# A new order for an attention stage, with three small steps of its first head pair put behind that pair's low parts

## The chip, the cores and the metric

The kernel runs on one core of a Trainium2 chip. The metric is the device time of one launch, in microseconds (us). The median of three runs before the change is 432.57 us (430.47 to 432.88).

The core has five engines that each work through their own list of instructions in the order in which the program was built, and wait for one another by semaphores: PE (matrix products and transposes), ACT (activations, copies, casts), DVE (elementwise work and reductions), POOL (elementwise work, constants, and transfers with computed addresses) and SP, which here only issues transfers. A long wait at the head of a list holds up all that stands behind it.

## The reference, cut to what matters

Three parts follow each other, all in float32:

```python
# 1. attention with a linear memory: B=2, H=8 heads, S=576 rows, D=64
scores = scale * q @ k.T ; causal ; a = softmax(scores) ; local = a @ v
q_p = where(q > 0, q, exp(q) - 1) + 1
mem = (q_p @ M_prev) / (q_p @ z_prev + 1e-6)
x = sigmoid(beta) * mem + (1 - sigmoid(beta)) * local       # 1152 tokens x 512

# 2. a mixture of 8 experts: each token goes to its best expert, at most 288 each
e = argmax(x @ w_gate) ; x = gate_w * relu(x @ w1[e]) @ w2[e]

# 3. a gated block
out = ((x @ w_a) * (x @ w_b)) @ w_out
```

## The kernel before, in words

**Work and stages.** The first stage holds the attention, the gate, and all of the expert with most tokens of the first batch. A branch on the counts follows, and the second stage computes the other experts and the gated block. Numbers are split into a high and a low part, and a product of two such numbers is three products on PE.

**The attention.** Heads are taken in pairs, eight pairs numbered 0 to 7. For each pair n the steps are: turn the queries (PE, step `qt`, line 428, into a PSUM tile `psS`), write their high part (ACT, `qh`, line 452) and low part (DVE, `ql`, line 466), a rectified copy (ACT, `qr`, line 457) and an exponential (ACT, `qe`, line 462) for the memory; POOL caps the exponential (`qm`, line 480) and adds the two (`qp`, line 486). Keys are turned (`kt`, line 428) and split (`kh`, line 494 on ACT; `kl`, line 498 on DVE). From pair 1 on, POOL copies parts side by side (`dq`, lines 513 to 517; `dk`, line 522) and SP moves the rest between partitions (`d`, line 505). `mm` (line 527) are the memory's products.

Each pair has five score tiles (n, 0) to (n, 4), of growing width. A tile goes through scores `S` (PE, lines 568 and 584), minimum and mask `M` (DVE, line 600), exponential `E` (ACT, line 620), transposes `T` (PE, line 635), copies out of PSUM `V` (ACT, lines 646 and 652), products with the values `P` (PE, lines 662 and 699), a turn back `X` (line 673, after the copy `os` of line 667) and the final scaling on DVE. There are two `psS` tiles in all: turned queries, turned keys, memory products and scores share them. Where ACT and DVE both read one PSUM tile, the build makes the second engine wait for the first.

**Small constants** (lines 365 to 375, step `small`): ACT takes the exponential of beta, DVE makes gate factors from it in four short instructions (lines 367 to 370), PE turns z, and DVE copies it into the memory's operand `mb` (line 374). The first `mm` needs it.

**What sets the order.** `Plan` (line 111) holds every step with an engine, a cost, what it follows, a key and the tiles it takes. `run` (line 150) plays the steps against these costs; of those that could start about first on an engine it takes the one with the least key. A key is the pair number plus the entries of `KEYS` (line 23) for that kind of step; `late` is how long after its end a step's result counts as there. Instructions are then emitted in that order, so the table sets the order of every engine's list. The order of the second stage comes from another table.

**Other traffic of the first stage.** Ten steps `z` (line 1100) clear the token buffer `xs_d` and the output in DRAM from SP; the first also fills `id_d` (line 422), 128 x 9 elements of 4 bytes. For batch 0, after pair 3, the gate's steps choose experts (`g1` to `g4`, lines 719 to 808), weigh the rows (line 781) and scatter them into `xs_d` (`g5`, line 813, on POOL). The first expert's tokens come back as `x0t` (line 951, SP).

Of the kernel before, what the change touches and what calls it, by code (L numbers as in the profile page):

```python
# [19 lines left out]

ABUFS = 3
SVB = 3
KEYS = dict(E=502, E_=221, F=-302.1, F_=64, L=118.7, M=-967.5, M_=566.5, N=-316.3, N_=50.2, O=-50.5, O_=-139, P=675.4,
            P_=-121.7, S=327, S_=188.6, T=-56.2, T_=-185.4, V=-77.6, V_=-123.1, X=-248.6, X_=66.4, consts=613.8,
            cv=-172.7, d=-43.2, e1=-207.9, e2=269, ec=1026.2, eh=-418.9, ep=113.4, ex=-759.2, ey=332.5, g1=274.3,
            g1_=-394.9, g1b=-306.3, g1b_=-110.1, g2=67.8, g2_=-153, g2b=51.5, g2b_=-136.7, g3=-413.3, g3_=-237.4,
            g4=-39.8, g4_=118, g4b=-451.8, g4b_=-214.9, g5=18.9, ge=-74.6, ge_=-163.6, gw=687.7, gw_=40.6, kh=-4.2,
            kl=149.6, kt=-65.6, last=69.9, mm=-247.7, mm_=1082, mn=-147.5, mo=188.3, mo_=401, pad0=-71.5, pad1=18.1,
            pb=101.2, pw=3.2, px=-43.8, qd=64.4, qe=-113.3, qh=-114.8, ql=-307.9, qm=31.9, qp=-222.9, qr=158.8,
            qt=-196.2, tc=219.1, tot=410.5, tr=-407.9, w=221.9, w_=92.1)  # L30
GK = 0.0
AHEAD_ = 0.132
CHANGE = 0.25
UNITS = [0, 1, 2, 3, 4]
ON_DVE = []
# [161 lines left out]
def fused_kernel(  # L197
# [256 lines left out]
    def q_relu(n):  # L454
        d = st[n]
        d["ph"] = ap2.tile([128, 128 * NT], F32, tag="ph", name="ph", bufs=1)
        nc.scalar.activation(out=d["ph"][:, 0:S], in_=d["qT"], func=AF.Relu)

    def q_exp(n):
        d = st[n]  # L460
        d["eq"] = ap2.tile([128, S], F32, tag="eq", name="eq", bufs=1)
        nc.scalar.activation(out=d["eq"], in_=d["qT"], func=AF.Exp)
# [6 lines left out]
    def q_stack(n):  # L469
        for h in range(2):  # L470
            me = slice(64 * h, 64 * h + 64)
            to = slice(64 * h, 64 * h + 64)
            src = st[n]["s"][me, 1, 128 * NF_:S] if n else st[n]["d"][me, h, 1, 128 * NF_:S]
            nc.gpsimd.tensor_copy(out=qd[sched.got["qd", n][1]][me, to], in_=src)
            if n == 0:
                nc.gpsimd.tensor_copy(out=qd[2][me, to], in_=st[n]["d"][me, h, 0, 128 * NF_:S])

    def q_min(n):
        eq = st[n]["eq"]
        nc.gpsimd.tensor_scalar(out=eq, in0=eq, scalar1=1.0, scalar2=None, op0=ALU.min)  # L480
# [507 lines left out]
    def work(name, engine, cost, do, after=(), key=(0, None), takes=(), uses=(), late=None, mode=0):  # L988

        at_, what = key  # L990
        keys = [] if what is None else [what] + ([what + "_"] if at_ >= LAST * UP and what + "_" in KEYS else [])
        meta.append((at_, keys, name))
        missing = [a for a in after if a not in op]
        assert not missing, (name, missing)
        op[name] = sched.add(engine, cost, do, [op[a] for a in after], at_ + sum(KEYS[k_] for k_ in keys), takes, uses,
                             LATES[engine] if late is None else late, 0, mode)

    def there(name, takes=(), late=0.0):
        work(name, "SP", 0.0, lambda: None, key=(-99, None), takes=takes, late=late)
# [9 lines left out]

    for n in range(min(2, len(pairs))):  # L1010
        for j, w in enumerate("qkv"):
            there(("load", n, w), [(w, (w, n))], (5.2, 7.9, 8.5, 9.5, 10.5, 11.5)[3 * n + j])
    there("d0", [("d", ("d", 0))])
    work("at first", "POOL", 5.5, lambda: None, (), (-99, None))
    for name, cost, do in (("last", 1.9, last_tile_constants), ("pad1", 1.2, lambda: padding(1)),
                           ("pad0", 1.2, lambda: padding(0)), ("consts", 3.6, gate_constants)):
        work(name, "POOL", cost, do, ["at first"], (0, name))
    there("zr", late=9.0)
    work("small", "PE", 0.2, small_constants, ["zr"], (-6, None), [("C", "small")], late=0.4)
    ZP = 10  # L1020
    for n, (b, p) in enumerate(pairs):
        at_ = n * UP
        if n > 1:
            for w in "qkv":
# [3 lines left out]
             [("q", n)])  # L1028
        work(("qh", n), "ACT", 0.531 if n else 1.06, lambda n=n: q_high(n), [("qt", n)], (at_, "qh"), (),
             [("qT", n), ("s", n)])  # L1030
        work(("qr", n), "ACT", 0.531, lambda n=n: q_relu(n), [("qt", n)], (at_, "qr"), (), [("qT", n), ("ph", n)])
        work(("qe", n), "ACT", 0.531, lambda n=n: q_exp(n), [("qt", n)], (at_, "qe"), (), [("qT", n), ("eq", n)])
        work(("ql", n), "DVE", 0.669 if n else 1.34, lambda n=n: q_low(n), [("qh", n)], (at_, "ql"), (),
             [("qT", n), ("s", n)])
        work(("qd", n), "POOL", 1.1, lambda n=n: q_stack(n), [("ql", n), "last"], (at_, "qd"), [("qd", ("qd", n))], [("s", n)])
        work(("qm", n), "POOL", 1.75, lambda n=n: q_min(n), [("qe", n)], (at_, "qm"), (), [("eq", n)])
        work(("qp", n), "POOL", 1.45, lambda n=n: q_phi(n), [("qm", n), ("qr", n)], (at_, "qp"), (),
             [("eq", n), ("ph", n)])
        work(("kt", n), "PE", 0.111 * NT, lambda n=n: k_turn(n), [("load", n, "k"), ("qt", n)], (at_, "kt"),
             [("S", ("kT", n))] + ([] if n else [("C", "stir2")]), [("k", n)])  # L1040
        work(("kh", n), "ACT", 0.531, lambda n=n: k_high(n), [("kt", n), ("qh", n)], (at_, "kh"), (),
             [("kT", n), ("s", n)])
        work(("kl", n), "DVE", 0.669, lambda n=n: k_low(n), [("kh", n)], (at_, "kl"), (), [("kT", n), ("s", n)])
        ready = [("ql", n), ("kl", n)]
        if n:
            work(("dq", n), "POOL", 2.75, lambda n=n: q_beside(n), [("qh", n), "pad0", "pad1"], (at_, "d"), [("d", ("d", n))], [("s", n)])
# [182 lines left out]
    if FAST:  # L1229
        if WA0:  # L1230
            for n, half in enumerate("sd"):
                def words_ahead(n):
                    c = sched.got["wa", n]
                    held_cells["raw", ("ff", "a", 0), n] = "raw", len(raws) + 2 * n + c[1]
                    load_words(raw_half(*c), w_a[:, 0:512], n)

                work(("wa", n), "SP", 2.92, lambda n=n: words_ahead(n), [("qt", LAST), ("d", LAST)], (tk, "pw"),
                     [(half, ("wa", n))], late=2.0)
        for j in range(NF):
            def block_ahead(j):  # L1240
                c = held_cells["raw", ((PRE_R, 0), PRE_R, 1, j)] = sched.got["pre", j]
                load_block(raws[c[1]], PRE_R, 1, j)

            work(("pre", j), "SP", 2.92, lambda j=j: block_ahead(j), ["rank"] + [("lo", NF + j_, 1) for j_ in range(NF)],
                 (tk, "pb"), [("raw", ("pre", j))], late=2.0)

        def tokens_ahead():
            c = sched.got["prex"]
            held_cells["xs", (PRE_R, 0)] = "raw", len(raws) + c[1]
            load_tokens(token_rows(raw_half(*c)), PRE_R, 0, 160 if PRE_R == NBIG - 1 else SW, nc.sync)  # L1250

        work("prex", "SP", 1.0, tokens_ahead, ["rank"] + [("g5", t) for t in range(L0, NTT)], (tk, "px"), [("s", "prex")],
             late=2.0)
        work("end", "", 0.0, lambda: None, ["prex", "totals", ("e", "yl", KD - 1)] + [("pre", j) for j in range(NF)] +
             [("wa", n) for n in range(2 * WA0)], (tk, None), (),
             ["prex"] + [("pre", j) for j in range(NF)] + [("wa", n) for n in range(2 * WA0)])
# [601 lines left out]
```

## Time and profile before

| what | us |
|---|---|
| median of three runs | 432.57 |
| the profiled execution | 430.72 |
| its span, first to last instruction | 428.9 |
| first scores of pair 0 begin | 10.78 |
| first scores of pair 2 begin | 47.78 |
| last product of the first stage begins | 177.19 |
| first work of PE in the second stage | 181.91 |

The profiled execution is 1.8 us longer than its span, and 1.85 us shorter than the median. PE is busy 398.1 us of the span, DVE 267.0, ACT 206.8 and POOL 103.9. Times in the rows are counted from the start of the span. In a row of the timeline the first number is the start, the second the time from the first to the last of the merged instructions, and what stands in brackets is how long the engine had been idle and what ended that.

### The profile page before, as it was taken

How to read it: one execution, taken by the hardware profiler on the slowest of the kernel's cores; microseconds unless marked ns; L12 is line 12 of the kernel's file. 1: busy time of each engine (PE TensorE's matmuls, PEld its weight loads, DVE VectorE, ACT ScalarE, POOL GpSimd, SP SyncE). 2: the span in 40 equal slices, each digit the busy share in tenths (PEclk: the TensorE clock that was granted, in tenths of full speed). 3: DMA queues.
4: the chain of work that ended last, by engine and by line, in shares of the span. 5: the costliest groups of instructions: out<-in, count | busy, mean ns of one | idle time of the engine just before them, and what ended most of it. 6: DMA issues, size and time to landing. Idle time of an engine off the chain costs nothing.

```text
span 428.9 us, 7838 instructions
## 1 busy us (share of the span) xinstructions
PE 398.1 (93%) x2860; PEld 348.3 (81%) x2860; DVE 267.0 (62%) x640; ACT 206.8 (48%) x451; POOL 103.9 (24%) x181
## 2 busy tenths in 40 slices
PE   5699889999989999589999989999999999999993
PEld 5678778887778999588998878898778987878892
DVE  5668678568997486256720128899957679743231
ACT  4388689687896452055711135354643354122010
POOL 6486745552830003300000000005700000000302
PEclk9699999999999997969999999999999999999998
DMA  5549899861996001779998999945960000000201
GB/s 134 131 106 138 172 297 252 244 199 54 307 288 232 2 3 59 250 277 387 387 385 314 378 397 407 383 166 135 165 127 2 0 2 1 0 2 0 97 4 62
DMA packets 59910, 74.46 MB, mean 174 GB/s; under 512 B 33955, under 2 KB 33955, under 8 KB 59856
## 3 DMA queue, kind: packets, MB, share of 16 engines
q1 hardware_dynamic: 58016, 70.48, 53.4%
q0 software_dynamic: 1632, 3.31, 2.3%
q8 instruction: 26, 0.43, 0.5%
q14 instruction: 28, 0.23, 0.2%
q10 hardware_dynamic: 208, 0.01, 0.0%
HBM read 58.75 MB, written 11.64 MB: 164 GB/s over the span
## 4 chain that ended last, share of the span: by engine, by line
PE 64%; DVE 8%; POOL 8%; issue 7%; DMA 6%; ACT 4%; ACTq 0%; SPq 0%; POOLq 0%
PE bank L954 10%; PE bank L955 9%; PE bank L956 9%; PE bank L1687 4%; PE bank L1688 4%; PE bank L1689 4%; PE bank L1547 3%; DMA id_d<-far 3%; PE bank L1454 3%; PE psB L954 2%; DVE sv L600 2%; PE psB L956 2%; PE bank L1490 2%; PE psB L955 2%; DMA raw<-in_moe_w_dram 2%
## 5 line engine op out<-in xcount | busy, mean ns | idle before, releaser
L954 PE MATMUL bank<-x,part 128*128 128x512 f32 (+1 forms) x192 | 66.7, 348 | 0.4 <-ACT x L966 0.4
L955 PE MATMUL bank<-x,part 128*128 128x512 f32 (+1 forms) x192 | 66.6, 347 | 0.0
L620 ACT ACTIVATE a<-sv,mn 128x128 f32<-128x128 f32 (+4 forms) x72 | 41.7, 584 | 17.9 <-DVE mn L600 17.2
L813 POOL DMA_INDIRECT id_d<-tid,dsi x10 | 13.6, 1362 | 116.6 <-DVE dsi L907 113.9
L954 PEld LDWEIGHTS bank<-x,part 128*128 128x128 f32 x192 | 36.1, 188 | 5.0 <-issue 0.6
L955 PEld LDWEIGHTS bank<-x,part 128*128 128x128 f32 x192 | 36.1, 188 | 4.2
L600 DVE CUSTOM_DVE_ANT_0 sv<-psS,mask 128x128 f32<-128x128 f32 (+4 forms) x72 | 34.4, 515 | 5.7 <-PE psS L584 4.1
L635 PE MATMUL psB<-ident,a 128*128 128x128 f32 x200 | 30.9, 278 | 2.7 <-ACT a L620 2.6
L956 PE MATMUL bank<-x,part 128*128 128x512 f32 (+1 forms) x96 | 33.3, 347 | 0.0
L956 PE MATMUL bank<-x,xt 128*128 128x512 f32 (+1 forms) x96 | 33.3, 346 | 0.0
L635 PEld LDWEIGHTS psB<-ident,a 128*128 128x128 f32 x200 | 23.5, 143 | 6.0 <-ACT a L620 4.3
L966 ACT CAST part<-u 128x1024 fp32r<-128x1024 f32 x18 | 18.7, 1050 | 18.2 <-DVE u L1371 14.9
L969 DVE TENSOR_TENSOR x<-bank,x 128x160 f32 (+3 forms) x12 | 4.2, 367 | 36.6 <-ACT x L966 36.6
L652 ACT COPY at<-psB 128x512 f32<-128x512 f32 (+2 forms) x48 | 23.6, 510 | 6.4 <-PE psB L635 6.3
L1663 ACT COPY c<-bank 128x512 f32<-128x512 f32 (+1 forms) x24 | 11.8, 499 | 25.7 <-PE bank L956 21.4
L1666 DVE TENSOR_TENSOR c<-c,bank 128x512 f32<-128x512 f32 (+1 forms) x24 | 13.8, 577 | 16.0 <-PE bank L956 11.0
L813 POOL DMA_INDIRECT out_dram<-c,ids x4 | 4.0, 988 | 80.8 <-DVE c L1697 79.0
L966 ACT CAST a<-c 128x512 fp32r<-128x512 f32 (+1 forms) x12 | 6.4, 534 | 35.4 <-DVE c L1666 28.8
L662 PE MATMUL psC<-at,ldv 128*64 128x256 f32 (+1 forms) x192 | 20.0, 350 | 0.5 <-ACT at L652 0.4
L813 POOL DMA_INDIRECT xs_d<-x,di x10 | 10.4, 1036 | 41.2 <-DVE ggt L774 37.0
L956 PEld LDWEIGHTS bank<-x,xt 128*128 128x128 f32 x96 | 18.0, 188 | 2.1
L956 PEld LDWEIGHTS bank<-x,part 128*128 128x128 f32 x96 | 18.0, 188 | 2.1
(281 smaller groups left out, 1081.9 us busy)
## 6 DMA issues: line engine op xcount, KB each, us to landing
raw<-in_moe_w_dram SPq DMA_DIRECT2D x16, 1024.0 KB, 8.2
raws<-in_moe_w_dram SPq DMA_DIRECT2D x6, 1024.0 KB, 10.6
rawd<-in_moe_w_dram SPq DMA_DIRECT2D x6, 1024.0 KB, 13.6
xs_d<-h SPq DMA_DIRECT2D x10, 512.0 KB, 4.8
raw<-in_moe_w_b_dram SPq DMA_DIRECT2D x4, 1024.0 KB, 13.8
d<-s SPq DMA_DIRECT2D x14, 288.0 KB, 4.0
rawd<-in_moe_w_a_dram SPq DMA_DIRECT2D x3, 1024.0 KB, 19.0
raws<-in_moe_w_out_dram SPq DMA_DIRECT2D x3, 1024.0 KB, 12.4
```

The costliest lines, as they stand in the source:

```text
L600: nc.vector.tensor_tensor_reduce(out=o, in0=i0, in1=i1, scale=1.0, scalar=3.0e38, op0=ALU.add, op1=ALU.min, accum_out=mn[:M])
L620: nc.scalar.activation(out=st[u, "a"][:M, h, 0:W], in_=sv[:M, 0:W], func=AF.Exp, scale=-1.0, bias=mn[:M], **more)
L635: nc.tensor.transpose(pt[:kr, M * j:M * j + M], a_t[:M, h, 128 * kt:128 * kt + kr], ident[:M, :M])
L652: eng(out=st[n, a, "at"][:, h0:h0 + nh, 0:i + 1, c0:c0 + 128], in_=pt[:, 0:m * 128].rearrange("p (h k m) -> p h k m", h=nh, m=128))
L662: nc.tensor.matmul(po[64 * h:64 * h + 64, c0:256], lhsT=vt[:, kt, h, 0:D], rhs=at_[:, h, kt, c0:256], start=kt == 0, stop=kt == 2 * a + 1)
L813: ins = nc.gpsimd.indirect_dma_start(out=out_[:, :], out_offset=bass.IndirectOffsetOnAxis(ap=idx, axis=0), in_=in_, in_offset=None, bounds ...
L954: nc.tensor.matmul(out_, lhsT=wh, rhs=xh, start=first, stop=False)
L955: nc.tensor.matmul(out_, lhsT=wh, rhs=xl, start=False, stop=False)
L956: nc.tensor.matmul(out_, lhsT=wl, rhs=xh, start=False, stop=last)
L966: nc.scalar.copy(out=to, in_=src)
L1687: nc.tensor.matmul(o, lhsT=g[:, 0, ts_], rhs=wh[:, m, :], start=m == 0, stop=False)
L1688: nc.tensor.matmul(o, lhsT=g[:, 0, ts_], rhs=wl[:, m, :], start=False, stop=False)
```

## The change

Three edits, all in the first stage's steps.

1. For pair 0, `qr` and `qe` now also follow `ql` and `kh`, and the step `small` follows `kl` (before, it came first of all, with key -6). In the source the steps of `qr`, `qe`, `qd`, `qm` and `qp` stand behind `kl`.
2. Planning figures: the keys of pair 0 count as there at 7.2 instead of 7.9, the result of `small` 2.5 instead of 0.4 after its end, and the step that loads tokens for the second stage has cost 1.6 and 3.5 after it, instead of 1.0 and 2.0.
3. All values of `KEYS` and `AHEAD_` are new.

```diff
-            qt=-196.2, tc=219.1, tot=410.5, tr=-407.9, w=221.9, w_=92.1)
+            qp=-218.7, qr=-108.5, qt=-332.6, tc=405.9, tot=85.8, tr=1033.4, w=515.2, w_=-76.2)
-AHEAD_ = 0.132
+AHEAD_ = 0.023
...
-            there(("load", n, w), [(w, (w, n))], (5.2, 7.9, 8.5, 9.5, 10.5, 11.5)[3 * n + j])
+            there(("load", n, w), [(w, (w, n))], (5.2, 7.2, 8.5, 9.5, 10.5, 11.5)[3 * n + j])
-    work("small", "PE", 0.2, small_constants, ["zr"], (-6, None), [("C", "small")], late=0.4)
...
-        work(("qr", n), "ACT", 0.531, lambda n=n: q_relu(n), [("qt", n)], (at_, "qr"), (), [("qT", n), ("ph", n)])
-        work(("qe", n), "ACT", 0.531, lambda n=n: q_exp(n), [("qt", n)], (at_, "qe"), (), [("qT", n), ("eq", n)])
...
+        first = [("ql", 0), ("kh", 0)] if n == 0 else []
+        work(("qr", n), "ACT", 0.531, lambda n=n: q_relu(n), [("qt", n)] + first, (at_, "qr"), (), [("qT", n), ("ph", n)])
+        work(("qe", n), "ACT", 0.531, lambda n=n: q_exp(n), [("qt", n)] + first, (at_, "qe"), (), [("qT", n), ("eq", n)])
...
+        if n == 0:
+            work("small", "PE", 0.2, small_constants, ["zr", ("kl", 0)], (-6, None), [("C", "small")], late=2.5)
...
-        work("prex", "SP", 1.0, tokens_ahead, ["rank"] + [("g5", t) for t in range(L0, NTT)], (tk, "px"), [("s", "prex")],
-             late=2.0)
+        work("prex", "SP", 1.6, tokens_ahead, ["rank"] + [("g5", t) for t in range(L0, NTT)], (tk, "px"), [("s", "prex")],
+             late=3.5)
```

What it moves is shown at three places.

**The start.** ACT, from the high part of pair 0's queries (L452) to its first score tiles (L620); before:

```order
L452 ACTIVATE d_76<-psS 64x576 x2
L462 ACTIVATE eq<-psS 128x576
L457 ACTIVATE ph<-psS 128x576
L494 CAST s_74<-psS 128x576
L366 ACTIVATE rg<-bet 128x8
L620 ACTIVATE a,sums<-sv,mn 128x128 x2
```

and now:

```order
L452 ACTIVATE d_76<-psS 64x576 x2
L494 CAST s_74<-psS 128x576
L462 ACTIVATE eq<-psS 128x576
L457 ACTIVATE ph<-psS 128x576
L620 ACTIVATE a,sums<-sv,mn 128x128
L366 ACTIVATE rg<-bet 128x8
```

The keys' high part (L494) has moved from fourth to second place, and beta's exponential (L366) between the two halves of the first score tile. DVE at the same place, before:

```order
L466 SCALAR_TENSOR_TENSOR d_76<-psS,d_76 64x576 x2
L367 TENSOR_SCALAR rg<-rg 128x8
L368 RECIPROCAL rog<-rg 128x8
L369 TENSOR_SCALAR rog<-rog 128x8
L370 RECIPROCAL rog<-rog 128x8
L374 COPY mb<-psC 64x8 x2
L498 TENSOR_TENSOR s_74<-psS,s_74 128x576
L600 ISA sv,mn<-psS,mask 128x128
```

and now:

```order
L466 SCALAR_TENSOR_TENSOR d_76<-psS,d_76 64x576 x2
L498 TENSOR_TENSOR s_74<-psS,s_74 128x576
L600 ISA sv,mn<-psS,mask 128x128
L600 ISA mn 128x1
...
L367 TENSOR_SCALAR rg<-rg 128x8
L368 RECIPROCAL rog<-rg 128x8
L369 TENSOR_SCALAR rog<-rog 128x8
L370 RECIPROCAL rog<-rog 128x8
L374 COPY mb<-psC 64x8 x2
L600 ISA sv,mn<-psS,mask 128x256
```

The constants (L367 to L374) no longer stand ahead of the keys' low part (L498), but between the minima of tiles (0, 0) and (0, 1).

**The first clearing transfers.** SP's list around them (`d_76<-s_74` is the move of pair 2, `ldv_82` its values), before:

```order
L281 DMA ldk_80<-in_k_dram 128x4x64 x2
L284 DMA ldk_80<-in_k_dram 64x2x64
L417 DMA xs_d<-h_97 128x2x512
L422 DMA id_d<-far 128x9x1
L505 DMA d_76<-s_74 64x1152 x2
L281 DMA ldv_82<-in_v_dram 128x4x64 x2
```

and now:

```order
L281 DMA ldk_80<-in_k_dram 128x4x64 x2
L284 DMA ldk_80<-in_k_dram 64x2x64
L505 DMA d_76<-s_74 64x1152 x2
L417 DMA xs_d<-h_97 128x2x512
L422 DMA id_d<-far 128x9x1
```

The move of pair 2 stands ahead of the clearing now, and three clearing steps follow each other behind it; the loads of pair 5 and the move of pair 3 come behind these.

**The gate of batch 0.** POOL's list around the five scatters (L813), before (pair 7's copies, `d_77`):

```order
L517 COPY qz_99<-s_75 64x64
L522 COPY d_77<-s_75 64x576 x2
L813 DMA xs_d<-x_95,di 2560x512 x5
L480 TENSOR_SCALAR eq<-eq 128x576
L485 MEMSET ph 128x64
```

and now (pair 6's copies, `d_76`):

```order
L486 TENSOR_TENSOR ph<-eq,ph 128x576
L474 COPY qd_138<-s_74 64x64 x2
L813 DMA xs_d<-x_95,di 2560x512 x5
L522 COPY d_76<-s_74 64x576 x2
L474 COPY qd_139<-s_75 64x64 x2
```

The scatters have moved from behind the last copy of pair 7 to ahead of the last copy of pair 6. On SP the load of `x0t` stands accordingly earlier, behind the first block of the first expert's weights and ahead of the second.

PE's list has the same products, all in all, up to the first scores of pair 2, in another order: all transposes and products of pair 0 now stand ahead of the scores of pair 1, and so do pair 2's turned queries and keys. At the first stage's end, 96 instead of 72 products of the first expert follow the last count of the gate (L840).

## Rows read from the trace of the kernel before

**Rows 1.** Windows: stretch, then busy time (instructions) by engine, granted clock, DMA.
```profile
10.00:20.00 10.00, 6.47 (x33) 6.03 (x33) 5.81 (x22) 3.68 (x13) 3.62 (x11) 0.66 0.62 137
20.00:30.00 10.00, 8.86 (x63) 7.52 (x63) 6.57 (x23) 8.09 (x22) 9.26 (x36) 1.00 0.50 121
40.00:47.78 7.78, 6.33 (x55) 4.63 (x53) 4.38 (x14) 5.50 (x13) 3.56 (x7) 1.00 0.92 61
47.78:177.50 129.72, 123.61 (x952) 111.22 (x952) 95.34 (x353) 85.92 (x219) 49.26 (x73) 0.97 0.60 186
```
**Rows 2.** Timeline of the start, pair 0 up to its first score tiles.
```profile
5.97 1.30 ACT L452 ACTIVATE d<-psS 64x576 fp32r<-64x576 f32 x2 [3.66 <-PE psS L428]
7.97 1.54 DVE L466 SCALAR_TENSOR_TENSOR d<-psS,d 64x576 fp32r<-64x576 f32 x2 [2.23 <-ACT eq L462]
9.54 0.65 ACT L457 ACTIVATE ph<-psS 128x576 f32<-128x576 f32 x1 [1.61 <-DVE d L466]
10.35 1.41 POOL L486 TENSOR_TENSOR ph<-eq,ph 128x576 f32<-128x576 f32 x1 [0.44 <-ACT ph L457]
10.87 1.37 DVE L367 TENSOR_SCALAR rg<-rg 128x8 f32<-128x8 f32 x1 [1.36 <-ACT rg L366]
12.51 0.22 DVE L369 TENSOR_SCALAR rog<-rog 128x8 f32<-128x8 f32 x1
13.35 0.76 DVE L498 TENSOR_TENSOR s<-psS,s 128x576 fp32r<-128x576 f32 x1
14.17 2.08 PE L584 MATMUL psS<-s,d 128*128 128x256 f32 x8 [2.65 <-DVE s L498]
16.28 0.42 DVE L600 CUSTOM_DVE_ANT_0 sv<-psS,mask 128x256 f32<-128x256 f32 x1 [0.77 <-PE psS L584]
```
**Rows 3.** Timeline, 20 to 37 us, of ACT, POOL and PE.
```profile
20.58 0.59 ACT L652 COPY at<-psB 128x512 f32<-128x512 f32 x1
24.20 0.62 ACT L620 ACTIVATE a<-sv,mn 128x384 f32<-128x384 f32 x1 [1.22 <-DVE mn L600]
27.66 0.19 ACT L620 ACTIVATION_READ_ACCUMULATOR a<-sv,mn 128x1 f32 x1
20.21 1.38 POOL L513 CAST d<-s 64x576 fp32r<-64x576 f32 x2 [6.03 <-ACT s L452]
23.20 1.40 POOL L522 CAST d<-s 64x576 fp32r<-64x576 f32 x2
24.68 1.65 POOL L480 TENSOR_SCALAR eq<-eq 128x576 f32<-128x576 f32 x1
27.61 0.65 PE L584 MATMUL psS<-d 128*128 128x256 f32 x2
29.89 0.71 PE L428 MATMUL psS<-ident,ldq 128*128 128x128 f32 x5
36.73 1.28 PE L699 MATMUL psC<-ldv,ats 128*128 128x130 f32 x10
```
**Rows 4.** Transfers of `d` in 30 to 60 us; then SP's timeline.
```profile
DMA to landing us min/median/max: 3.2/4.6/11.6
34.85 0.42 SPq L422 DMA_DIRECT2D id_d<-far  x1
35.37 1.70 SPq L505 DMA_DIRECT2D d<-s  x2
```
**Rows 5.** PE's waits, 34 to 178 us: total, times, longest; then POOL's timeline.
```profile
PE psB L963 <- DMA x0t<-xs_d: 0.6, 1, 0.6
111.61 1.22 POOL L813 DMA_INDIRECT xs_d<-x,di  x1 [0.30 <-POOL d L522]
117.43 0.93 POOL L813 DMA_INDIRECT xs_d<-x,di  x1 [0.30 <-issue]
```
**Rows 6.** Timeline where the first stage ends and the second begins.
```profile
181.91 1.18 PE L963 MATMUL bank<-ident,raws 128*128 128x128 f32 x8 [4.43 <-DMA raws<-xs_d]
183.19 1.12 ACT L1357 ACTIVATE u<-raws 128x1024 f32<-128x1024 f32 x1 [5.28 <-issue]
```

More of the change, by code (lines that the diff above doesn't have):

```diff
@@ L22 @@
 SVB = 3
[L23 to L29, printed above, removed]
-            qt=-196.2, tc=219.1, tot=410.5, tr=-407.9, w=221.9, w_=92.1)
+KEYS = dict(E=358.5, E_=-162.9, F=106.7, F_=666.7, L=287, M=53.6, M_=13.7, N=522.1, N_=145.3, O=359.6, O_=226.3,
+            P=-164.7, P_=256.1, S=-149.4, S_=15.6, T=-1591.6, T_=-456.1, V=-393.3, V_=109, X=-194.3, X_=48.6,
+            consts=-164.4, cv=74.2, d=367.5, e1=-19.3, e2=-393.9, ec=593.7, eh=-473.9, ep=217.9, ex=-549.8, ey=1062.5,
+            g1=-230.9, g1_=101.4, g1b=-581.4, g1b_=-295.8, g2=-626.4, g2_=58.7, g2b=23.9, g2b_=-159, g3=552.3,
+            g3_=374.5, g4=55.4, g4_=153.3, g4b=225.1, g4b_=-121.5, g5=-56.2, ge=-221.1, ge_=-183.6, gw=21.5,
+            gw_=281.2, kh=135.1, kl=279.9, kt=-525, last=212.3, mm=-309.9, mm_=600.3, mn=-389.7, mo=-169.2, mo_=182.3,
+            pad0=-342.4, pad1=142.4, pb=212.8, pw=447.3, px=448.3, qd=-106.2, qe=-205, qh=-404.9, ql=53.6, qm=-451.4,
+            qp=-218.7, qr=-108.5, qt=-332.6, tc=405.9, tot=85.8, tr=1033.4, w=515.2, w_=-76.2)
 GK = 0.0
-AHEAD_ = 0.132
+AHEAD_ = 0.023
 CHANGE = 0.25
@@ L1030, in fused_kernel @@
              [("qT", n), ("s", n)])
-        work(("qr", n), "ACT", 0.531, lambda n=n: q_relu(n), [("qt", n)], (at_, "qr"), (), [("qT", n), ("ph", n)])
-        work(("qe", n), "ACT", 0.531, lambda n=n: q_exp(n), [("qt", n)], (at_, "qe"), (), [("qT", n), ("eq", n)])
         work(("ql", n), "DVE", 0.669 if n else 1.34, lambda n=n: q_low(n), [("qh", n)], (at_, "ql"), (),
              [("qT", n), ("s", n)])
[L1035 to L1038, printed above, removed]
         work(("kt", n), "PE", 0.111 * NT, lambda n=n: k_turn(n), [("load", n, "k"), ("qt", n)], (at_, "kt"),
@@ L1043, in fused_kernel @@
         work(("kl", n), "DVE", 0.669, lambda n=n: k_low(n), [("kh", n)], (at_, "kl"), (), [("kT", n), ("s", n)])
+        first = [("ql", 0), ("kh", 0)] if n == 0 else []
+        work(("qr", n), "ACT", 0.531, lambda n=n: q_relu(n), [("qt", n)] + first, (at_, "qr"), (), [("qT", n), ("ph", n)])
+        work(("qe", n), "ACT", 0.531, lambda n=n: q_exp(n), [("qt", n)] + first, (at_, "qe"), (), [("qT", n), ("eq", n)])
+        work(("qd", n), "POOL", 1.1, lambda n=n: q_stack(n), [("ql", n), "last"], (at_, "qd"), [("qd", ("qd", n))], [("s", n)])
+        work(("qm", n), "POOL", 1.75, lambda n=n: q_min(n), [("qe", n)], (at_, "qm"), (), [("eq", n)])
+        work(("qp", n), "POOL", 1.45, lambda n=n: q_phi(n), [("qm", n), ("qr", n)], (at_, "qp"), (),
+             [("eq", n), ("ph", n)])
+        if n == 0:
+            work("small", "PE", 0.2, small_constants, ["zr", ("kl", 0)], (-6, None), [("C", "small")], late=2.5)
         ready = [("ql", n), ("kl", n)]
```

## The prediction, before the kernel was run

> **What bounds the kernel now.** I read the page's table of engines first: PE is busy 398.1 of 428.9 us, so time can only come from stretches in which PE stands still or runs at its lower clock. The windows say where these are in the first stage [rows 1]. From 10 to 20 us PE is busy 6.47 us and its granted clock is 0.66: if it was at its upper level (2.4 GHz) otherwise, it spent 0.34 / 0.5 = 6.8 us of these ten at the lower one (1.2 GHz). From 20 to 30 us it idles 1.14 us beside an ACT that is busy 8.09; from 40 to 47.78 it idles 1.45. In all the rest of the stage, 129.72 us, it idles only 129.72 - 123.61 = 6.1 us. So there are some 12 us to be won at most, nearly half of them ahead of 48 us, and the branch behind the stage besides.
>
> The timeline shows what holds the start [rows 2]. The closing products of the first score tiles start at 14.17, after 2.65 us of idling for the keys' low part (L498). That stands on DVE at 13.35, behind the constants, which run from 10.87; their first instruction waited for beta's exponential on ACT. ACT was late because its rectified copy (L457, 9.54) waited 1.61 us for the queries' low part (L466), as the two may not read the PSUM tile together; L466 in turn had waited 2.23 us for the exponential of the same tile.
>
> **Edit 1, the start.** The queries' high part ends at 5.97 + 1.30 = 7.27 [rows 2]. Nothing of ACT stands ahead of the low part any more: 7.27 + 1.54 = 8.81. The keys' high part follows on ACT (taken as long as L457, 0.65: about 8.5, since the keys' turn must land first, estimate), and the keys' low part ends at 8.81 + 0.76 = 9.6. The closing products can start there, 14.17 - 9.6 = 4.5 us earlier.
>
> What moved is not gone. The exponential and the rectified copy now follow L466: 8.8 to 10.1 on ACT. POOL caps (1.65, [rows 3]) from 9.5 and adds (L486, 1.41) from about 11.2 to 12.6. Tile (0, 0) is done by 10.5, its minimum by 11.0, the first half of its exponential by 11.4; beta's exponential comes next, so the constants start on DVE at about 11.6. Their first instruction took 1.37 us where it lay beside L486; it falls beside L486 again, so I take 1.37: it ends at about 13.0. The rest of the constants took 13.35 - 12.24 = 1.1: the minimum of (0, 1) starts at 14.1 instead of 16.28, 2.2 us earlier. Half of the 4.5 is given back here; if the first instruction took only the 0.22 of L369, it would be 1.15 less, 3.4 earlier.
>
> The Trainium skill (SBUF — State Buffer, Who interferes with whom) says that DVE and POOL share one port pair under an exclusive lock, and that a DVE operation in a two-port mode is held for a whole POOL instruction. L367's 1.37 fits, but L369 is the same operation and took 0.22 while POOL was at work; by the rule taken strictly L369 would be held by what POOL has next, some 0.5 more, and my sum below would be 3.1 instead of 3.6.
>
> From there ACT sets the pace, since the new order lets it take pair 0's tiles (0, 1) to (0, 3) ahead of pair 1's high part. From 14.5: exponentials of (0, 1) about 1.1 (an estimate, below those of (0, 2)), a copy 0.4, a copy 0.59, and for (0, 2), (0, 3) and a copy between them 27.85 - 24.20 = 3.65 at most [rows 3], one more copy 0.5 and the high part 0.65: together 6.5 to 6.9, so 21.0 or a little later. Before, POOL's work on that high part started at 20.21 and the keys' copy (L522) ended at 24.60. Now POOL takes 23.20 - 20.21 = 3.0 for the queries, then 1.65 + 1.41 for pair 1's cap and sum and some 0.6 for small fills and copies (estimate), which are put ahead of L522, and then 1.40: 21.0 + 8.1 = 29.1. Pair 1's first scores started at 27.61 and now can't before 29.1, 1.5 later. But PE has work for that time: pair 2's turns (0.71 twice) and pair 0's last products (1.28), 2.7 us in all, which stood behind those scores. The lead there is 2.7 - 1.5, less some 0.2 for transposes that have moved the other way: 1.0 us. **Term: -1.0.** Bounds: +1.0 (POOL or ACT another 2 us later than reckoned) and -4.5 (the whole head start kept). The clock is inside these bounds: if PE's first ten microseconds are fed without the gap before 14.17, its 6.8 us at the lower level could become 3.4 at the upper one; I count none of that, since PE still waits for minima there.
>
> **New order, the first clearing.** SP issued the fill of small elements (id_d, 34.85) just ahead of pair 2's move (35.37), and the slowest move of the stretch took 11.6 us against a median of 4.6 [rows 4]. 35.4 + 11.6 = 47, and pair 2's first scores start at 47.78 behind 1.45 us of PE idling. Now the move goes first. **Term: -0.8**, about half of that idling; bounds 0 (the wait was another, or passes to pair 3's move or pair 5's loads, now behind the clearing) and -1.5.
>
> **New order, the rest of the stage.** 6.1 us of idling are left there [rows 1], in small waits on many steps. One goes surely: the tokens of the first expert (x0t, 0.6, [rows 5]) come some 18 us earlier, with the scatters. Of the remainder I take a fifth, since the order spreads the gate's work on DVE over a longer time. **Term: -1.8**; bounds -4 and +3 (the scatters, below).
>
> **The end of the stage.** PE's first work behind the branch waited 4.43 us by the row, for a load of tokens, but ACT shows 5.28 us there with no releaser [rows 6]: the branch itself costs about that much. 24 more products behind the last count give the scatter and the token load some 3 us more, which buys nothing if the branch is what is waited for. **Term: 0**; bounds -1 and +0.5. The second stage's order is the same. The planning figures themselves cost nothing; they act through the order.
>
> **Sum.** -1.0 - 0.8 - 1.8 = -3.6. The profiled execution took 430.72, so 427.1; it stood 1.85 below the median of 432.57, and on that footing the forecast is 429.0.
>
> **The rivals.**
>
> *More is kept.* L367 runs at 0.2 to 0.3, and the earlier first pair feeds PE at the upper clock: 3 us more, -6.6, 426.0. For it: L369's 0.22, and a clock of 0.66 that leaves 3.4 us on the table. Against: L486 falls on the same place, and ACT and POOL still stand between pair 0 and pair 1.
>
> *Given back.* The start's lead ends at ACT and POOL before pair 1, the clearing's wait passes to pair 3, and the idling of the rest changes its place only: within about 0.5 of no change, 432.6. For it: POOL is busy 9.26 of 10 us from 20 to 30 [rows 1], and its list there has grown no shorter. Against: PE has 2.7 us of work to lay over it.
>
> *Slower.* The five scatters took POOL from 111.61 to 117.43 + 0.93 = 118.36, 6.75 us [rows 5], behind the last copy of pair 7. Now they stand ahead of pair 6's last copy and of all of pair 7's copies, and they wait for row weights that DVE makes. My count of what PE has between the gate's choice and pair 6's scores is about 18 us, against some 12 for the chain of weights (3, an estimate), scatters (6.75), pair 6's copy (1.40) and its move's start (1): 6 us to spare. If the weights come over 6 us late, which an order with much else on DVE can do, every further microsecond is PE's. At 9 us late for pair 6, and again for pair 7, that is 3 + 3 = 6 us, less the 3.6: +2.4, 435.0. Against: POOL is busy only 49.26 of 129.72 us there [rows 1].
>
> **How the numbers follow.** Forecast 429.0: 0.48. More is kept, 426.0: 0.15. Given back, 432.6: 0.24. Slower, 435.0: 0.13. A measurement of this kernel tells some 0.5%, 2.2 us, from no change: faster is below 430.4, slower above 434.7. The forecast's own range is 427 to 431; 0.45 of its 0.48 lie in faster, with the whole of the second case, 0.15: 0.60. Same has the third case's most, 0.23, and 0.03 of the forecast: 0.26. Slower: 0.13 and 0.01. The range goes from 424.5, which leaves out the outer part of the second case (0.05), to 433.5, which leaves out the fourth (0.13): 0.8.
>
> **What would show it.** Start: closing products of (0, 0) at about 9.6; L367 long again beside L486, and the minimum of (0, 1) at about 14.1; pair 1's first scores at 29 with pair 2's turns ahead of them. Pair 2's first scores at about 46.0: there both orders have the same products behind them, so the lead can be read at that place (1.8), and the pair's move lands in 3 to 5 us. No wait of PE for x0t, and none of pair 6's or 7's scores for POOL's copies. The first stage's last product near 173.6 instead of 177.2, and the gap behind it still about 4.7 us. I am wrong if the lead at pair 2 is near 0 or above 4; if the scores of pair 6 wait behind the scatters; or if the gap at the branch takes back what the stage won. A granted clock well above 0.66 from 10 to 20 us would speak for the second case.

## The result and the profile after

The changed kernel took 437.0 us, the median of four runs (436.11 to 439.18), against 431.89 for four of the kernel before (430.47 to 432.88): a ratio of 1.0128 (of the means), with a 95% interval of 1.0079 to 1.0178. The forecast was 429.0, faster. Timed once more in another session, 12 runs beside 35 of the kernel before, it stood at 1.0034 (0.9999 to 1.0069). So the change won nothing. Whether it costs 0.3% or 1.3% the two sessions don't agree on, but both exclude the forecast's 0.992.

Two quantities help to read this. Each run has its span and its mean granted clock. Span times clock counts a microsecond at the upper level (2.4 GHz) whole and one at the lower level (1.2 GHz) half. I call this "work and waiting", and the rest of the span "lost to the clock". The second is the most that the lower level can have cost, since a wait at that level is halved as well. In the session of the repeat they average 416.7 and 15.4 us for the kernel before, and 422.0 and 11.6 for the changed one: some 5 us more work and waiting, some 4 us less lost. The four runs of the first session average 422.2 and 13.4. These averages, and those below, leave out runs more than 1.5% above the fastest of their kernel.

Three places tell the story. The start, in the changed kernel's timeline (start, duration, engine, line, operation; in brackets the idle time before it and what ended it):

```profile
8.93 0.76 DVE L498 TENSOR_TENSOR s<-psS,s 128x576 fp32r<-128x576 f32 x1
9.74 1.69 PE L584 MATMUL psS<-s,d 128*128 128x256 f32 x12 [1.81 <-DVE s L498]
11.84 1.06 DVE L367 TENSOR_SCALAR rg<-rg 128x8 f32<-128x8 f32 x1 [0.45 <-ACT rg L366]
14.01 0.42 DVE L600 CUSTOM_DVE_ANT_0 sv<-psS,mask 128x256 f32<-128x256 f32 x1
27.82 1.38 PE L527 MATMUL psS<-mb,ph 128*128 128x130 f32 x10 [1.82 <-POOL ph L486]
33.10 0.49 PE L584 MATMUL psS<-d 128*128 128x256 f32 x2 [0.86 <-issue]
46.29 0.48 PE L584 MATMUL psS<-d 128*128 128x256 f32 x2
```

Against [rows 2] the closing products start 4.4 us earlier and the minimum of (0, 1) 2.3 us earlier; pair 2's first scores (46.29) stand 1.5 us ahead of those in [rows 1]. That lead is not the same in every execution: eight other profiles with the same first steps have 45.38 to 46.83, and the other profile that starts as the kernel before (to_pair3_old) has 49.26, not 47.78. Then the windows, by the columns of [rows 1]:

```profile
10.00:20.00 10.00, 8.22 (x46) 7.20 (x46) 5.85 (x24) 5.54 (x20) 6.24 (x15) 0.83 0.62 135
46.29:181.58 135.29, 125.48 (x954) 111.65 (x953) 96.48 (x354) 85.87 (x218) 50.02 (x74) 0.96 0.61 182
```

PE is busy 8.22 us instead of 6.47 in the first window, and its clock is 0.83 instead of 0.66. But the stretch from pair 2's scores to the end of the stage, with the same products, takes 135.29 us instead of 129.72: PE idles 9.8 us there instead of 6.1, and is busy 1.9 longer (the clock is at the lower level from 97.5 to 100.9 and from 152.1 to 158.9 us; before, from 158.8 to 165.7 alone). The waits of PE in that stretch (total, times, longest) are small and many; the first five:

```profile
PE psB L635 <- ACT a L620: 1.6, 4, 0.7
PE psB L963 <- DMA x0t<-xs_d: 1.5, 1, 1.5
PE psS L584 <- ACT ph L457: 1.0, 1, 1.0
PE psC L791 <- DVE accs L762: 0.9, 1, 0.9
PE psB L954 <- DVE xt L969: 0.9, 1, 0.9
```

Last the branch, in the timeline again:

```profile
182.14 1.81 SPq L940 DMA_DIRECT2D raw<-in_moe_w_dram  x2
185.47 1.23 PE L963 MATMUL bank<-ident,raws 128*128 128x128 f32 x8 [3.89 <-issue]
189.03 1.12 ACT L1359 ACTIVATE u<-raws 128x1024 f32<-128x1024 f32 x1 [7.02 <-issue]
190.38 3.04 PE L1456 MATMUL bank<-d,raw 128*128 128x160 f32 x10 [3.68 <-ACT d L966]
```

PE is back after 3.89 us instead of 4.43 [rows 6], but ACT after 7.02 instead of 5.28. PE's first long products then wait 3.68 us for ACT, where they had waited 1.45 (from 184.54 on). Four differences make up that of the spans, 435.1 - 428.9 = 6.2: lead at pair 2 -1.5, rest of the stage +5.6, gap of PE -0.5, and second wait with what else differs behind it +2.6.

### The profile page after: what moved, and what is told of

It reads as the page before. It is cut to its first block, busy times and chain, and to the rows that moved or that the text cites. A ratio compares the mean times of both kernels' runs of the same rounds, so it can differ in the third digit from the quotient of the medians.

```text
span 435.1 us, 7867 instructions
## 1 busy us (share of the span) xinstructions
PE 399.8 (92%) x2860; PEld 348.7 (80%) x2860; DVE 267.2 (61%) x640; ACT 206.4 (47%) x451; POOL 103.8 (24%) x181
## 4 chain that ended last, share of the span: by engine, by line
PE 66%; DVE 10%; issue 9%; ACT 8%; DMA 4%; POOL 2%; SPq 0%; ACTq 0%; DVEq 0%; POOLq 0%
PE bank L954 9%; PE bank L955 9%; PE bank L956 9%; PE bank L1689 4%; PE bank L1690 4%; PE bank L1691 4%; ACT a L620 3%; PE bank L1549 3%; PE psS L584 3%; PE bank L1456 3%; DVE sv L600 2%; PE psC L735 2%; PE psB L635 2%; PE bank L1492 2%; DMA raw<-in_moe_w_dram 2%
## 5 line engine op out<-in xcount | busy, mean ns | idle before, releaser
L620 ACT ACTIVATE a<-sv,mn 128x128 f32<-128x128 f32 (+4 forms) x72 | 41.9, 584 | 13.5 <-DVE mn L600 13.5
L813 POOL DMA_INDIRECT id_d<-tid,dsi x10 | 13.6, 1362 | 118.4 <-DVE dsi L907 115.7
L600 DVE CUSTOM_DVE_ANT_0 sv<-psS,mask 128x128 f32<-128x128 f32 (+4 forms) x72 | 34.4, 514 | 5.6 <-PE psS L584 4.8
L635 PE MATMUL psB<-ident,a 128*128 128x128 f32 x200 | 32.2, 283 | 2.2 <-ACT a L620 1.6
L1668 DVE TENSOR_TENSOR c<-c,bank 128x512 f32<-128x512 f32 (+1 forms) x24 | 13.8, 577 | 16.1 <-PE bank L956 11.1
L813 POOL DMA_INDIRECT out_dram<-c,ids x4 | 3.9, 986 | 80.3 <-DVE c L1699 78.5
L662 PE MATMUL psC<-at,ldv 128*64 128x256 f32 (+1 forms) x192 | 20.9, 364 | 0.0
L1363 DVE TENSOR_SCALAR u<-u 128x1024 f32<-128x1024 f32 x18 | 12.4, 690 | 10.7 <-ACT u L1359 10.6
```

The costliest lines, as they stand in the source:

```text
L600: nc.vector.tensor_tensor_reduce(out=o, in0=i0, in1=i1, scale=1.0, scalar=3.0e38, op0=ALU.add, op1=ALU.min, accum_out=mn[:M])
L620: nc.scalar.activation(out=st[u, "a"][:M, h, 0:W], in_=sv[:M, 0:W], func=AF.Exp, scale=-1.0, bias=mn[:M], **more)
L635: nc.tensor.transpose(pt[:kr, M * j:M * j + M], a_t[:M, h, 128 * kt:128 * kt + kr], ident[:M, :M])
L662: nc.tensor.matmul(po[64 * h:64 * h + 64, c0:256], lhsT=vt[:, kt, h, 0:D], rhs=at_[:, h, kt, c0:256], start=kt == 0, stop=kt == 2 * a + 1)
L813: ins = nc.gpsimd.indirect_dma_start(out=out_[:, :], out_offset=bass.IndirectOffsetOnAxis(ap=idx, axis=0), in_=in_, in_offset=None, bounds ...
```

## The experiments

The changed table alone can't be taken apart, since every key acts on every engine. So the two emitted orders were spliced: up to a named step the list of one kernel, behind it the other's order for all that remained. Apart from the order such a kernel is the changed one (to_pair3_old: the one before).

```diff
-    sched.run()
+    follow(sched, op)      # emits the steps as ORDER lists them
+ORDER = [...]
```

**The start alone.** The changed order up to the first scores of pair 2, ("S", (2, 0)), then that of before.

> The changed kernel's order up to the first scores of pair 2, then the order of before for all that is left. In the trace of the changed kernel those scores start at 46.29 instead of 47.78 us. Theory (the start gains what it shows, the loss lies behind it): 431.9 - 1.5 = 430.4, and the branch's gap on ACT as before, 5.3 us. Rival (the gain at the start is given back by what follows in any order, or the start is itself what costs): 431.9 or above, and PE's lead gone by pair 4.

Measured: 0.9912 (0.9872 to 0.9953), 430.53 us beside 434.48. The lead is there and stays:

```profile
10.00:20.00 10.00, 8.13 (x56) 7.21 (x56) 7.05 (x30) 6.63 (x23) 6.58 (x15) 1.00 0.63 138
45.38:173.95 128.57, 123.74 (x954) 111.02 (x952) 95.18 (x354) 86.08 (x218) 49.43 (x74) 0.97 0.63 185
```

From 45.38 on the stage takes 128.57 us, 1.2 less than before. The clock from 10 to 20 us is 1.00. That is not this order's alone: of the nine profiles with these first steps this one has no lower level in its first 50 us, five have 3.4 us of it at about 16 to 20 us, and three have 3.4 us at about 28 to 32; the two that start as the kernel before have 6.8 us, from 12 to 19.

The start is a gain, larger than my -1.0 and -0.8 together. By the averages it is all clock: 11.0 us are lost to it instead of 15.2, and work and waiting stands at 417.7 instead of 416.6. The profile alone would not show the gain: the lead is 2.4 us at pair 2 and 3.5 at the end of the stage, but the span is only 0.4 us shorter (428.5). The gap at the branch is 5.57 us instead of 4.43, and the rest takes 249.0 us from PE's first work instead of 247.0, with 3.4 us at the lower level near 255 us that the kernel before doesn't have there.

**Up to pair 3, and the complement.** The changed order up to ("S", (3, 4)), then before's; and the other way round.

> The changed kernel's order up to the last score tile of pair 3 (68.66 us there, 69.82 before), then the order of before. Theory (the loss lies behind pair 3, at the gate of batch 0 and later): 431.9 - 1.2 = 430.7. Rival (the many small waits of 0.3 to 0.5 us in pairs 2 and 3 cost it): 432.5 or above.

> The complement: the order of before up to the last score tile of pair 3, then the changed kernel's order. Theory (the parts add): 437.0 + 1.2 = 438.2. Rival (the changed order is slow only behind its own start, as its pairs come in another phase): between 432 and 436.

Measured: 0.9981 (0.9939 to 1.0024) and 1.0052 (1.001 to 1.0093). With pairs 2 and 3 in the changed order most of the start's gain is gone (the two intervals overlap a little); with the later part alone changed the kernel is slower. The loss is spread over the stage, not in one place.

**The gate's work of batch 0.** In the changed kernel the choice of experts and the row weights stand between pair 5's and pair 6's splits on DVE. Two orders move them: gate_later puts `g3`, `ge` and the first `gw` behind ("kl", 6) and `g4` and `g4b` behind ("O", 4, 1); gate_split does the same, but puts `g4b` and the weighing of the rows behind ("M", (5, 1), 1).

> The changed kernel with the choice of experts of batch 0 (the five steps g3, ge, gw, g4, g4b) moved: g3 to gw behind the low part of pair 6's keys, g4 and g4b behind the turn-out of pair 4's second group. In the changed kernel g3 holds DVE from 91.72 to 95.3 us ahead of pair 6's low part of the queries, ACT waits 2.13 us behind that, PE 0.95 and 1.05 us, and its clock is at the lower level from about 97.4 to 102. Theory (this block is the largest single loss): pair 5's first scores at about 95.1 instead of 97.37, no lower clock there, and 437.0 - 2.5 = 434.5. Rival (the block costs its 3.6 us wherever DVE does it, or the wait passes to the minima behind it): 437.0.

> As gate_later, but the weighing of rows (L781) and the positions (L800 to L808) wait behind the minima of tile (5, 1), and the positions stand ahead of the weighing. In gate_later these stood ahead of the minima, which came at 106.99 us, 4.6 us after the scores, and PE waited 1.0 and 1.75 us. Theory (what counts is what stands ahead of the pair's own steps on DVE, not the size of the gate's block): those two waits go, and the time is 1.5 to 3 us under gate_later's 438.6, 1.003 to 1.008 of before. Rival (the block's DVE time is lost wherever it stands): 1.010 to 1.014.

Measured: 1.0124 (1.0087 to 1.0161) and 1.0137 (1.0082 to 1.0193, six runs): neither helps. What gate_later was to remove is this, in the changed kernel's timeline:

```profile
93.01 2.35 DVE L762 TENSOR_TENSOR accs<-accs,oh 128x8 f32<-128x8 f32 x5
95.29 0.74 DVE L466 SCALAR_TENSOR_TENSOR s<-psS,s 128x576 fp32r<-128x576 f32 x1
96.13 0.65 ACT L462 ACTIVATE eq<-psS 128x576 f32<-128x576 f32 x1 [2.13 <-DVE ggt L772]
97.37 0.72 PE L584 MATMUL psS<-d 128*128 128x256 f32 x2 [1.05 <-ACT ph L457]
```

Pair 6's low part (L466) comes behind the gate's five additions, ACT's exponential of the same `psS` tile behind it, and PE's scores of pair 5 wait for that tile. gate_later's timeline shows that wait cut to a quarter, and two others in its place (the first row is another matter, below):

```profile
62.70 0.36 PE L584 MATMUL psS<-d 128*128 128x256 f32 x1 [1.75 <-DMA d<-s]
97.89 0.50 PE L584 MATMUL psS<-d 128*128 128x256 f32 x2 [0.27 <-ACT ph L457]
105.63 0.44 PE L673 MATMUL psC<-ident,os 128*128 128x128 f32 x2 [1.02 <-DVE gp L802]
106.99 0.42 DVE L600 CUSTOM_DVE_ANT_0 sv<-psS,mask 128x256 f32<-128x256 f32 x1
107.81 1.01 PE L584 MATMUL psS<-d 128*128 128x384 f32 x2 [1.75 <-DVE mn L600]
```

The gate now stands ahead of the minima of (5, 1), and PE waits for those. That pair 5's scores are still no earlier than 97.37 comes mostly from ahead of the edit: PE waited 1.75 us for pair 3's move there, which it didn't in the changed kernel's profile (in the repeat's it did, 1.07 us). In gate_split the gate stands ahead of the final scaling (L547), and PE waits longer in one place:

```profile
107.35 1.19 PE L584 MATMUL psS<-d 128*128 128x512 f32 x2 [2.85 <-DVE x L547]
```

The wait is passed on, whatever it is put behind: the rival of that expectation held.

**Casts out of the gate's way.** POOL's copies of pair 6's high part lie beside the gate's additions. dq_later puts ("dq", 6) behind ("qm", 6), on POOL alone.

> The changed kernel with one step of POOL moved: pair 6's copies of the queries (L513 to L517) behind that pair's cap (L480), which waits for the exponential; all other engines keep their lists. In the changed kernel the five additions of the gate's count (L762, 128x8) take 2.35 us where L513 and L514 run on POOL beside them; 19 such additions with nothing on POOL beside them took 0.17 each. Theory (DVE is held for POOL's copies): the five take 0.9 to 1.0 us, and pair 5's first scores come about 1.4 us sooner than the 97.4 and 98.1 us of the two profiles; in time 0 to -1.4, which lies inside the interval. Rival (the additions are slow for another reason, as the PSUM tile they follow): 2.3 us again.

Measured: 1.0059 (1.002 to 1.0099). Its timeline:

```profile
93.50 0.97 DVE L762 TENSOR_TENSOR accs<-accs,oh 128x8 f32<-128x8 f32 x5
96.58 0.51 PE L584 MATMUL psS<-d 128*128 128x256 f32 x2 [0.65 <-ACT ph L457]
102.86 1.38 PE L527 MATMUL psS<-mb,ph 128*128 128x130 f32 x10 [1.73 <-POOL ph L486]
```

The five additions take 0.97 us instead of 2.35, and pair 5's scores start 0.8 us earlier than in the changed kernel. That POOL's copies had held the additions is shown. The time doesn't fall, and the last row shows one reason: the copies now stand ahead of POOL's sum of pair 6 (L486), and PE waits 1.73 us for that sum, a wait that the changed kernel doesn't have.

**The tail alone.** start_new's order up to ("S", (7, 4)), then the changed one. Beside it, on the same chip, the changed kernel itself.

> The order of start_new up to the last score tile of pair 7 and from there the changed kernel's order, so that only the end of the first stage and its branch are those of the changed kernel. Theory (the loss of the changed order lies in the gate of batch 0 and in the later tokens of the first expert, ahead of this place): 0.991 to 0.996 of before, ACT's gap at the branch 6.3 to 7.0 us with SP's weight loads ahead of PE's first work. Rival (the end of the stage, with the choice of experts of batch 1 inside the first expert's products, costs the most): 1.000 or above.

> The changed kernel itself, so that its times stand beside the others on one chip. The first comparison gave 1.0128 (1.0079 to 1.0178): 1.010 to 1.016 here. If run noise made much of that figure (it had four runs), 1.000 to 1.008.

Measured: 0.9943 (0.9903 to 0.9984) and 1.0034 (0.9999 to 1.0069). These two differ in the middle alone, from pair 2 to pair 7, so the middle costs about 0.0091 x 434 = 4 us. The tail is worth little: by start_new's interval it can't be told from nothing.

**Edit 1 alone.** The order of before, with `qe`, `qr` and `qm` of pair 0 behind ("kh", 0), and `small` behind ("M", (0, 0), 1).

> The order of before, with the first edit alone: pair 0's exponential, rectified copy and cap behind its keys' high part, and the small constants behind the minima of tile (0, 0). All else as before. Theory (the first edit by itself ends the wait for the keys' low part and keeps PE busy early, so that the lower clock from 12.1 to 18.9 us shortens): first closing products at 9.7 instead of 14.17 and most of what the order of the whole start gained (0.9912 of before): 0.991 to 0.996. Rival (the gain at the start is that of the new order of pair 0's tiles): within 0.997 to 1.003.

Measured: 0.9946 (0.9907 to 0.9985). By the times the edit wins without the new order. Its profile, an execution above its median (433.41 against 432.00), doesn't show where, but it shows a new wait:

```profile
9.50 1.68 PE L584 MATMUL psS<-s,d 128*128 128x256 f32 x12 [1.80 <-DVE s L498]
11.61 1.57 DVE L369 TENSOR_SCALAR rog<-rog 128x8 f32<-128x8 f32 x1
16.02 2.51 PE L527 MATMUL psS<-mb,ph 128*128 128x130 f32 x10 [4.68 <-DMA mb<-in_M_prev_dram]
49.76 0.80 PE L584 MATMUL psS<-d 128*128 128x256 f32 x2
```

The wait taken off the keys comes back as 4.68 us at the memory's products, and pair 2's first scores, at 49.76, have no lead over the kernel before (47.78, and 49.26 in to_pair3_old). The constants are not what they wait for: their last copy into `mb` (L374) ends at 13.64. It is the load of M_prev into `mb`, which SP issues at 11.89 here as in the kernel before. There, too, these products start no sooner, at 16.04. The changed order puts them behind others of pair 0, and so has work until that load is in.

**SP's weight loads held back.** At the branch, two small copies on SP (the second reads what the first wrote) are put ahead of the second stage's weight loads:

```diff
     load_tokens(...)
+    hold_queue(nc, drm, raw_half(*c))
+def hold_queue(nc, drm, loaded):
+    nc.sync.dma_start(out=t, in_=loaded[0:1, 0:64])
+    nc.sync.dma_start(out=u, in_=t)
```

> The changed kernel with two small copies on SP behind the token load that stands ahead of the branch, each waiting for the landing before it, so that SP passes the branch later and its weight loads start at about 186 instead of 182.1 us. Theory (in the changed kernel these loads start while ACT's instructions behind the branch are still being fetched, and so ACT starts 7.0 us after its last work instead of 5.3): ACT's gap 5.3 to 5.6, PE's wait behind it 2 instead of 3.7, 1.3 to 1.7 us less than the changed kernel in all. Rival (ACT's gap has nothing to do with these loads): gap 6.9 to 7.1, time the same or up to 3 us more, since the weights come later.

Measured: 1.0054 (1.0013 to 1.0095). Its timeline:

```profile
187.03 1.13 ACT L1359 ACTIVATE u<-raws 128x1024 f32<-128x1024 f32 x1 [3.99 <-DMA hold<-hold]
188.39 7.82 PE L1456 MATMUL bank<-d,raw 128*128 128x160 f32 x35 [1.44 <-ACT d L966]
189.22 1.39 SPq L940 DMA_DIRECT2D raw<-in_moe_w_dram  x2
```

With the loads behind ACT's return its gap is 3.99 us instead of 7.02, and PE's second wait is 1.44 instead of 3.68. (The row puts the end of ACT's gap down to the second copy, which no instruction reads.) Yet the time doesn't fall: the weights come 7 us later, and the second stage takes 250.0 us from PE's first work, against 248.9 in the repeat.

**Beta's part first.** Lines 366 to 370 taken out of `small_constants` and called before the first step, so that they run while PE still waits for the first loads: beta_first with start_new's order, before_beta_first on the kernel before with its own.

```diff
+    def beta_constants():
         ... (lines 366 to 370)
     def small_constants():
...
+    beta_constants()
     follow(sched, op)
```

> The order of start_new, with beta's exponential and its four short DVE instructions (L366 to L370) taken out of the small constants and issued ahead of the first step; beta lands at 5.2 us and ACT is idle until 6.4. DVE then has only the copy of z between the minima of tiles (0, 0) and (0, 1). Theory: minima of (0, 1) at 12.2 to 12.8 instead of 14.37 and 0.5 to 1.5 us less than start_new: 0.988 to 0.991 of before. Rival (ACT or the second psS tile paces pair 0, or the early exponential delays the queries' high part): 0.991 or above.

> The kernel before with its own order, and beta's exponential and the four short DVE instructions ahead of the first step: nothing else is moved. It takes the wait for beta's exponential out of the chain that ends in the keys' low part at 13.35. Theory (that wait and the constants are what the first edit removes): keys' low part at about 10.8 to 11.3, first closing products at 11.5 to 12 instead of 14.17, and about what the first edit alone gave: 0.992 to 0.997. Rival (the serial reading of the queries' tile by ACT and DVE is what matters, which stays): 0.998 to 1.002.

Measured: 0.987 (0.9829 to 0.9912, six runs), 426.72 us beside 432.15; and 0.9958 (0.9929 to 0.9987). beta_first beats both kernels. Its timeline and its window (the edit moves later lines down by two, so L602 is the L600 of above):

```profile
5.22 0.21 ACT L366 ACTIVATE rg<-bet 128x8 f32<-128x8 f32 x1 [2.91 <-DMA bet<-in_beta_dram]
5.66 0.51 DVE L367 TENSOR_SCALAR rg<-rg 128x8 f32<-128x8 f32 x1
12.58 0.42 DVE L602 CUSTOM_DVE_ANT_0 sv<-psS,mask 128x256 f32<-128x256 f32 x1
43.80 0.48 PE L586 MATMUL psS<-d 128*128 128x256 f32 x2
```

```profile
10.00:20.00 10.00, 9.44 (x69) 8.42 (x71) 6.66 (x29) 8.40 (x26) 7.42 (x17) 1.00 0.67 148
```

The minimum of (0, 1) comes 1.4 us earlier than in the changed kernel, pair 2's scores 2.5 earlier, and PE is busy 9.44 of the ten microseconds. In before_beta_first the memory's products wait for M_prev at the same 16.1 us as in edit1_only, and the clock from 10 to 20 us is 0.58. Pair 2's first scores start at 48.26, so here too the profile doesn't show where the 0.4% comes from:

```profile
16.13 2.51 PE L529 MATMUL psS<-mb,ph 128*128 128x130 f32 x10 [2.85 <-DMA mb<-in_M_prev_dram]
```

## Why the prediction was wrong

**The start: right in place, too small in worth.** Closing products at 9.74 (9.6 was forecast), L367 at 1.06 us (1.37), the minimum of (0, 1) at 14.01 (14.1), pair 2's scores at 46.29 (46.0). Pair 1's scores came at 33.10, not 29. The working had POOL's sum L486 about right, but not that pair 1's memory products, which need it, stand in PE's list ahead of those scores and of pair 2's turns: PE waited 1.82 us for it there, so the turns could not be laid over POOL's work. What I left out of the sum is the clock, "I count none of that". start_new alone is worth 0.9%, 3.8 us, in place of 1.8, and its lost clock fell by 4.2. The working had shown that 3.4 us were there to be had; "PE still waits for minima there" was no reason to take zero.

**The first clearing: the move as said, the wait not shown.** Pair 2's move has no landing in the changed kernel's trace; in start_new its two halves landed 3.3 and 4.5 us after their issue, where the slower half had taken 11.6. But the profile of the kernel before puts PE's idling just ahead of pair 2's scores down to a copy on ACT, not to the move:

```profile
47.23 0.44 PE L673 MATMUL psC<-ident,os 128*128 128x128 f32 x2 [1.01 <-ACT os L667]
```

So whether the -0.8 was won for the reason given stays open. Its bound of 0 named pair 3's move, and that came in two profiles of the changed order, as the 1.07 and 1.75 us above.

**The constants.** I chose 1.37 us beside L486, and 1.06 came; L367 ended with L486 (11.84 + 1.06 = 12.90, L486 at 11.44 + 1.43 = 12.87). In the kernel before it had outlasted L486 and ended with the memset behind it (12.24; POOL's L330 at 11.69 + 0.53 = 12.22), hence the 1.37. The strict reading of the Trainium skill's rule on the shared port pair (SBUF — State Buffer, Who interferes with whom) also held: L369 took 0.36 here, not 0.22, and ended, at 13.53, with the first of two memsets on POOL (L340, two in 1.20 us from 12.93). The 0.22 of [rows 2] on which I doubted the rule doesn't speak against it either: it ended at 12.73, and POOL's L333 beside it at 12.17 + 0.54 = 12.71. In edit1_only the same L369 took 1.57, beside L486 and the memset behind it, and ended with that memset (13.18 and 13.15).

**The step that failed: "New order, the rest of the stage", -1.8 with bounds -4 and +3.** It came to +5.6 in the profiled executions, and some +4 by tail_new against the changed kernel. I reckoned from the idle time that was there (6.1 us) and took a part of it as won; that a new order can make new idle time I had bounded only by the scatters. The lead at equal work of PE shows where it went: the time at which each kernel has done W us of products, minus the same for before. Each product counts with the time that its shape takes at the upper level, as fitted to these traces; the figures are estimates, good to some 0.3 us.

| W, us | 29 | 45 | 78 | 84 | 114 | 126 | 150 |
|---|---|---|---|---|---|---|---|
| changed kernel | -0.1 | -2.0 | -0.3 | +3.2 | +1.3 | +2.0 | +4.1 |
| the same, repeated | +0.4 | -1.4 | +0.4 | +2.8 | +0.5 | +1.3 | +4.8 |
| start_new | -1.1 | -3.0 | -2.8 | -2.8 | -3.5 | -3.5 | -3.5 |
| beta_first | -2.6 | -4.6 | -4.8 | -4.8 | -4.7 | -4.7 | -4.7 |

start_new makes its lead and holds it. The changed kernel has 1.4 to 2.0 us at pair 2 (W = 45), gives them up in pairs 2 to 5, and between W = 78 and 84 loses 2 to 4 us more, at the gate of batch 0: DVE's choice of experts ahead of pair 6's low part, as the rows above show. Part of that comes back by W = 114, and 3 to 4 us go between there and the end of the stage; what takes those is not shown. My own sentence, "the order spreads the gate's work on DVE over a longer time", named one of the places and drew the wrong sign. That the middle loses is shown by tail_new; that the gate is what costs there is read from the rows, and none of the three orders tried there made the kernel faster. Nor did x0t's wait go, which I called sure: it became 1.54 us. The tokens are issued at 113.53 instead of 121.73, 8.2 us earlier and not 18, and the products that need them were put earlier still.

**The slower rival was right on the side in the first session, but not for its reason.** It rested on five scatters on POOL that hold pair 6's copies; no wait of PE for a scatter or those copies is in the changed kernel's trace.

**The end of the stage, "0", bounds -1 and +0.5.** It measured +2.1 in the profile (-0.5 and +2.6). PE's gap shrank, but ACT's grew. Two sets of kernels show the pattern. Where SP's weight loads start some 3 us before PE's first work, ACT's gap is 6.33 to 7.02 us (the changed kernel, its repeat, to_pair3_old, gate_later, gate_split, dq_later, tail_new); where they start after it, 4.97 to 5.77 (before, start_new, to_pair3_new, edit1_only). sp_held held SP back and brought 3.99. That ACT's gap hangs on when SP passes the branch and starts its loads is thus shown. Whether it is the loads' traffic or SP's own passage isn't, as the two copies delay both, nor what ACT does in the gap. As sp_held's time didn't fall, it is no proof either that the gap is what the whole run pays: start_new and beta_first, with ACT's gap at 5.41 and 5.20 us, took 249.0 and 249.5 us from PE's first work too.

**What stays open.** The size of the loss, between 0.3% and 1.3%; which of the many small waits take the start's lead in pairs 2 to 5, and which cost the rest behind the gate, since no run took the loss of the middle away short of restoring the old order; where the edit alone and beta's part alone win their 0.5% and 0.4%; and how much of the difference between sessions is clock: single runs of before went from 429.56 to 440.13 us.

## What to carry to other kernels

In this stage the bounding engine idled 5% in many small waits, and a new order of the whole of it moved waits and made some 4 us of loss, more than the 1.8 forecast as gain. So take the local edit first and leave the rest in its order. Look at the granted clock when a start is tightened: here 6.8 us at the lower level became 3.4 or none, and the average loss to the clock fell by 4.2 us in start_new while work and waiting didn't fall. And when work is moved off a chain, look for what is late next (here M_prev's load, at which PE stood 4.68 us), and move what has no inputs from the chain, such as beta's constants, all the way to the front.

## What the runs showed of the hardware that was not expected

A 128x8 addition on DVE (L762) took 0.17 us where POOL was idle (all ten in the kernel before), and three of the changed kernel's took 0.54 to 0.67 beside POOL's casts of 64x576; a 128x40 comparison (L757) took 0.20 in the changed kernel and 1.06 in gate_later, beside POOL's addition L486. In these rows the time of such an instruction says more of what POOL does than of its own size. L369 ended with a memset on POOL as L367 did with an addition.

The gap of an engine at the branch isn't a constant: ACT's was 3.99 to 7.02 us in kernels with the same second stage, and went by when SP passed the branch and began to load the weights.

The same program's mean granted clock differs from run to run and takes its time along: two runs of before in one session had spans and clocks of 429.7 us at 0.972 and 434.7 us at 0.962.
